# Hash attention and a mixture of adapters on one core: x turned by TensorE for fourteen pairs, proj spread by two products, and a new list of steps

## The chip, the cores and the metric

The kernel runs on one core of one Trainium2 chip. The metric is the device time of one execution in microseconds (us), the median of several runs; smaller is better. The core has five engines that work at once and meet only at semaphores: TensorE (PE in the profile, its weight loads PEld), VectorE (DVE), ScalarE (ACT), GpSimd (POOL) and SyncE (SP), which here only issues transfers. Each engine carries out its own instructions strictly in the order in which they were written, so an instruction that waits holds up everything behind it on its engine.

## The reference

Four batches of eight heads, 768 positions, 64 numbers per head. Two queries and keys may see each other only where the signs of six projections (their hash codes) are equal; the rows that the attention gives are then the input x of a mixture of eight rank-16 adapters, of which each row uses two.

```
q_bits = einsum('bhsd,dk->bhsk', q, proj) > 0          # the same for k; proj is 64 x 6
mask   = q_bucket[:, :, :, None] == k_bucket[:, :, None, :]
scores = where(mask, q @ k.T / sqrt(64), -1e9)
attn   = softmax(scores) @ v                           # (4, 8, 768, 64)
x      = attn.transpose(0, 2, 1, 3).reshape(3072, 512)
logits = x @ w_gate                                    # 8 experts, the best two with softmax weights w
out    = x + sum over the two of  w * (x @ A[e]) @ B[e]
```

## The kernel before

**Pairs.** The 32 heads are worked off as sixteen pairs of two heads, four pairs to a batch. For a pair, the rows of q and k are loaded (`Lq`, `Lk`), cast to bf16 on POOL (`Nq`, `Nk`), and turned by the crossbar, a DMA that transposes (`Xq`, `Xk`, issued by SP), into a buffer `aug` of which there are three; the second head is shifted down to the first 64 partitions by POOL or DVE (`Sk`, `Sq`). In parallel DVE turns the 32 x 32 blocks of the same rows (`Tq`, `Tk`), PE multiplies them with `hst`, a spread copy of proj (`Ha`), DVE takes the signs (`G`), and SP writes them to DRAM (`W`) and reads them back (`Rd`) into rows 64 to 69 of `aug`. A score matmul then contracts over 70 rows: 64 of the head and six of codes, so that unequal codes push a score down.

**Scores and attention.** `Sc p s` fills one of three PSUM buffers of 1024 columns, `Ex p s` is the exp of it on ACT, nine to a pair and 144 in all. `Pv` multiplies the exps with v, `U` adds a small constant row, `Nr` divides and writes x, in float32. v is loaded, cast and summed by `Lv`, `Vc` and `Vs`, the last two on POOL. The last two pairs go in six smaller pieces, whose steps end in `l` (`Pvl`, `Nl`, `Xbl`, `Xpl`, `Xcl`).

**Adapters.** x of a pair is cast to bf16 on POOL (`Xb`, L490) and has to be turned. For pairs 0 to 7 PE turns it (`Xp`, six transposes at L500) and DVE copies it out of PSUM (`Xc`, L504); for pairs 8 to 13 the crossbar does both (`Xx`, L494). When the four pairs of a batch are turned, `Lg` gives logits and low-rank products, `Mx`, `Ge`, `Gw`, `Zm`, `Sr` the gates, `Zt`, `Zc`, `De`, `St` the result, `Ou` the store.

**The start.** Pair 0 has its own way: quarters of q and k are loaded (`L0`, two by SP, two by ACT's queue), turned by PE in float32 (`T0`), copied (`FC`, `CA`), and their codes are made directly (`HH` on PE with proj, `SG0` on DVE and ACT). `Lproj` loads proj twice by SP. `hst` spreads it by eight copies of 32 x 6 numbers on DVE (L221). A few matmuls on zeros (`warm`) stand at the beginning.

**Order.** `STEPS` is a list written out by hand or by a program; `run` calls each step in turn, and that fixes the order on every engine and in every queue. `BANKS` says which PSUM pool a tile uses: `s` (three buffers, the scores and the start's tiles), `v` and `m` (one each). No scheduler reorders anything.

Of the kernel before, what the change touches and what calls it, by code (L numbers as in the profile page):

```python
# [31 lines left out]
BANKS = """
tf0=v hh0=s tf1=m hh1=s tf2=v hh2=s tf3=m hh3=s warm=s s0_0=s s0_1=s s0_2=s s0_3=s s0_4=s s0_5=s s0_6=s s0_7=s
s0_8=s pv0_0=m pv0_1=v xt0=m hs1=m s1_0=s s1_1=s s1_2=s s1_3=s s1_4=s s1_5=s s1_6=s s1_7=s s1_8=s pv1_0=m
pv1_1=v xt1=m hs2=m s2_0=s s2_1=s s2_2=s s2_3=s s2_4=s s2_5=s s2_6=s s2_7=s s2_8=s pv2_0=m pv2_1=v xt2=m hs3=m
s3_0=s s3_1=s s3_2=s s3_3=s s3_4=s s3_5=s s3_6=s s3_7=s s3_8=s pv3_0=v pv3_1=m xt3=m lz0_0=m zt0_0=m dl0_0=m
dl0_1=m dl0_2=v lz0_1=m zt0_1=m dl0_3=m dl0_4=m dl0_5=m hs4=v s4_0=s s4_1=s s4_2=s s4_3=s s4_4=s s4_5=s s4_6=s
s4_7=s s4_8=s pv4_0=v pv4_1=v xt4=m hs5=m s5_0=s s5_1=s s5_2=s s5_3=s s5_4=s s5_5=s s5_6=s s5_7=s s5_8=s
pv5_0=v pv5_1=v xt5=v hs6=v s6_0=s s6_1=s s6_2=s s6_3=s s6_4=s s6_5=s s6_6=s s6_7=s s6_8=s pv6_0=v pv6_1=v
xt6=m hs7=m s7_0=s s7_1=s s7_2=s s7_3=s s7_4=s s7_5=s s7_6=s s7_7=s s7_8=s pv7_0=v pv7_1=m xt7=m lz1_0=m  # L40
zt1_0=m dl1_0=m dl1_1=m dl1_2=m lz1_1=m zt1_1=m dl1_3=m dl1_4=v dl1_5=m hs8=m s8_0=s s8_1=s s8_2=s s8_3=s
s8_4=s s8_5=s s8_6=s s8_7=s s8_8=s pv8_0=v pv8_1=v hs9=m s9_0=s s9_1=s s9_2=s s9_3=s s9_4=s s9_5=s s9_6=s
s9_7=s s9_8=s pv9_0=v pv9_1=v hs10=v s10_0=s s10_1=s s10_2=s s10_3=s s10_4=s s10_5=s s10_6=s s10_7=s s10_8=s
pv10_0=v pv10_1=v hs11=m s11_0=s s11_1=s s11_2=s s11_3=s s11_4=s s11_5=s s11_6=s s11_7=s s11_8=s pv11_0=v
pv11_1=m lz2_0=m zt2_0=m dl2_0=m dl2_1=m dl2_2=m lz2_1=m zt2_1=m dl2_3=v dl2_4=m dl2_5=v hs12=m s12_0=s
s12_1=s s12_2=s s12_3=s s12_4=s s12_5=s s12_6=s s12_7=s s12_8=s pv12_0=v pv12_1=v hs13=m s13_0=s s13_1=s
s13_2=s s13_3=s s13_4=s s13_5=s s13_6=s s13_7=s s13_8=s pv13_0=v pv13_1=v hs14=m hs15=v s14_0=s s14_1=s
s14_2=s s14_3=s s14_4=s s14_5=s s14_6=s s14_7=s s14_8=s s14_9=s s14_10=s s14_11=s s14_12=s s14_13=s s14_14=s
s14_15=s s14_16=s s14_17=s pvl0=m xtl0=s pvl1=v xtl1=m pvl2=m xtl2=s pvl3=s xtl3=s pvl4=m xtl4=s pvl5=s xtl5=s
lz3_0=s zt3_0=v dl3_0=v dl3_1=v dl3_2=v lz3_1=s zt3_1=s dl3_3=v lz3_2=m zt3_2=s dl3_4=s lz3_3=s zt3_3=s  # L50
dl3_5=m
# [4 lines left out]
Lq 1,Nq 1,Tq 1,Wt 2,Sc 0 0,Sc 0 1,Ex 0 0,T0 3,FC 3,CA 3 1,CA 2 1,CA 3 0,CA 2 0,Nq 2,Lk 3,Lk 2,Nk 2,Lv 0,Vc 0
Xk 1,Xq 1,hst,HH 2,SG0 2 0,SG0 2 1,Sc 0 2,Ex 0 1,Ex 0 2,HH 3,SG0 3 1,SG0 3 0,Ha 1,G 1,W 1,Lv 1,Sc 0 3,Sc 0 4
Sc 0 5,Ex 0 3,Ex 0 4,Sc 0 6,Ex 0 5,Ex 0 6,Sc 0 7,Sc 0 8,Xq 2,Tq 2,Tk 2,Sq 1,Ha 2,G 2,vones,Pv 0 1 4,Ex 0 7
Ex 0 8,Sk 1,Rd 1,Sc 1 0,Pv 0 0 4,Sc 1 1,Sc 1 2,Vs 0,U 0 0,Pv 0 0 5,Ex 1 0,Ex 1 1,Ex 1 2,Nk 3,Tk 3,Xk 2,Sk 2
Lq 3,Tq 3,Nq 3,Vc 1,Vs 1,Lv 2,Vs 2,W 2,Xk 3,Lq 4,Sk 3,Nq 4,Sq 2,Rd 2,Xq 3,Sc 1 3,Pv 0 0 0,Pv 0 0 1,Pv 0 0 2  # L60
# [636 lines left out]
```

## Time and profile before

| | before |
|---|---|
| median of 3 runs | 174.94 us (173.92 to 176.3) |
| the profiled execution | 175.81 us, of which the span from first to last instruction is 174.0 us |
| PE busy | 153.6 us, 88% |
| ACT busy | 142.2 us, 82% |
| DVE busy | 118.2 us, 68% |
| POOL busy | 101.9 us, 59% |
| mean granted TensorE clock | 0.938 |
| moved by DMA | 34.15 MB, 196 GB/s |

A row of groups names the line of the kernel, the engine, the operation, out<-in with their shapes and the count; behind the first bar stand the busy time of the group and the mean of one in ns, behind the second the idle time just before it and what ended it. A row of the timeline begins with its start and its length in us and ends with the idle time before it in brackets. A row of stages gives, for each engine, its busy us in the stage (and how many instructions started), then the granted clock (1.00 is full), the DMA share and GB/s.

### The profile page before, as it was taken

How to read it: one execution, taken by the hardware profiler on the slowest of the kernel's cores; microseconds unless marked ns; L12 is line 12 of the kernel's file. 1: busy time of each engine (PE TensorE's matmuls, PEld its weight loads, DVE VectorE, ACT ScalarE, POOL GpSimd, SP SyncE). 2: the span in 40 equal slices, each digit the busy share in tenths (PEclk: the TensorE clock that was granted, in tenths of full speed). 3: DMA queues.
4: the chain of work that ended last, by engine and by line, in shares of the span. 5: the costliest groups of instructions: out<-in, count | busy, mean ns of one | idle time of the engine just before them, and what ended most of it. 6: DMA issues, size and time to landing. Idle time of an engine off the chain costs nothing.

```text
span 174.0 us, 5211 instructions
## 1 busy us (share of the span) xinstructions
PE 153.6 (88%) x2098; PEld 103.3 (59%) x2098; DVE 118.2 (68%) x302; ACT 142.2 (82%) x168; POOL 101.9 (59%) x154
## 2 busy tenths in 40 slices
...
PEclk9998555799999999999999999999999999999995
...
GB/s 183 343 237 68 106 205 221 144 84 203 189 197 198 169 175 243 230 180 252 146 236 180 206 224 277 182 216 263 205 106 302 187 191 147 255 143 146 143 308 162
DMA packets 63075, 34.15 MB, mean 196 GB/s; under 512 B 48714, under 2 KB 61130, under 8 KB 63050
## 3 DMA queue, kind: packets, MB, share of 16 engines
...
q0 software_dynamic: 4832, 0.27, 5.2%
...
q8 instruction: 16, 0.26, 0.7%
...
## 4 chain that ended last, share of the span: by engine, by line
PE 40%; DMA 29%; DVE 14%; POOL 7%; issue 3%; SPq 3%; DVEq 1%; ACT 0%; POOLq 0%
PE s L426 18%; PE pv L462 9%; DMA aug<-nb 7%; DMA vn<-in_v_dram 6%; DMA nat<-in_q_dram 6%; DMA dr<-s 5%; PE hs L383 4%; DMA xT<-xb 3%; DVE R L370 3%; DMA aug<-dr 2%; PE lz L569 2%; PE pvl L526 2%; DVE x L634 2%; POOL nb L320 2%; DVE zm L600 2%
## 5 line engine op out<-in xcount | busy, mean ns | idle before, releaser
L435 ACT ACTIVATE P<-s 128x1024 bf16<-128x1024 f32 x144 | 135.2, 1049 | 14.5 <-PE s L426 14.3
L426 PE MATMUL s<-aug 70*128 70x512 bf16 (+3 forms) x426 | 84.9, 325 | 1.7 <-DMA aug<-dr 1.2
L462 PEld LDWEIGHTS <-P 128*128 128x128 bf16 x1008 | 42.8, 100 | 14.1 <-issue 4.1
L426 PEld LDWEIGHTS <-aug 70*128 70x128 bf16 x426 | 35.6, 101 | 22.8 <-issue 8.5
L462 PE MATMUL pv<-vb,P 128*128 128x65 bf16 x1008 | 46.8, 197 | 1.4 <-DVE ri L482 1.4
L370 DVE STREAM_TRANSPOSE R<-nat 128x768 f32<-128x768 f32 x30 | 28.7, 966 | 5.0 <-DMA nat<-in_q_dram 2.9
L320 POOL CAST nb<-nat 128x768 bf16<-128x768 f32 x30 | 24.7, 828 | 11.5 <-DMA nat<-in_q_dram 7.1
L262 POOL TENSOR_TENSOR vs<-vn 128x384 f32<-128x384 f32 x16 | 16.0, 1002 | 10.7 <-DMA vn<-in_v_dram 10.5
L634 DVE SCALAR_TENSOR_TENSOR x<-dl,rt,x 128x512 f32<-128x512 f32 x24 | 17.6, 742 | 2.4 <-PE dl L627 2.2
L383 PE MATMUL hs<-R,hst 128*32 128x192 f32 x240 | 14.1, 351 | 5.9 <-DVE hst L221 3.2
L490 POOL CAST xb<-x 128x768 bf16<-128x768 f32 x14 | 11.5, 824 | 10.2 <-DVE x L484 8.7
L256 POOL CAST vb<-vn 128x768 bf16<-128x768 f32 x16 | 13.5, 845 | 6.4 <-DMA vn<-in_v_dram 6.4
L359 POOL COPY aug<-aug 64x768 bf16<-64x768 bf16 x15 | 12.4, 824 | 7.4 <-DMA aug<-nb 6.7
L484 DVE TENSOR_TENSOR x<-pv,ri 128x384 f32<-128x384 f32 x28 | 15.6, 558 | 1.0
L383 PEld LDWEIGHTS hs<-R,hst 128*32 128x32 f32 x240 | 6.7, 113 | 10.9 <-issue 6.2
L482 DVE RECIPROCAL ri<-pv 128x6 f32<-128x6 f32 x28 | 5.2, 185 | 10.3 <-PE pv L462 5.6
L359 DVE COPY aug<-aug 64x768 bf16<-64x768 bf16 x15 | 8.6, 576 | 4.8 <-DMA aug<-nb 4.4
L390 DVE TENSOR_SCALAR sg<-hs 128x192 bf16<-128x192 f32 x15 | 5.4, 357 | 9.6 <-PE hs L383 9.5
L569 PE MATMUL lz<-wa,xT 128*128 128x136 bf16 x96 | 8.4, 223 | 2.2 <-DMA xT<-xb 1.8
L627 PE MATMUL dl<-Bcat,zT 128*128 128x512 bf16 x24 | 9.0, 381 | 0.7 <-DVE x L634 0.4
L450 PE MATMUL pv<-vb,eps 128*128 128x390 bf16 x28 | 9.5, 339 | 0.0
L569 PEld LDWEIGHTS <-xT 128*128 128x128 bf16 x96 | 6.4, 97 | 4.0 <-DMA xT<-xb 2.3
...
## 6 DMA issues: line engine op xcount, KB each, us to landing
...
```

Source lines behind the costliest of these rows:

```text
L256: self.nc.gpsimd.tensor_copy(out=self.vb[p % 3][:, :, 0:self.T, 0:self.D], in_=self.vn[p])
L262: nc.gpsimd.tensor_add(out=s3, in0=vn[:, :, 0:3, :], in1=vn[:, :, 3:6, :])
L320: self.nc.gpsimd.tensor_copy(out=t.rearrange("p t h d -> p h t d"), in_=self.nat[p, c].rearrange("p h (t d) -> p h t d", t=self.T))
L359: (self.nc.vector if (p, c) in SHIFT_DVE else self.nc.gpsimd).tensor_copy(out=a[0:64, :, 2 + c, :], in_=a[64:128, :, c, :])
L370: self.nc.vector.transpose(out=t, in_=self.nat[p, c])
L383: self.nc.tensor.matmul(out=hs[32 * j:32 * j + 32], lhsT=self.hstt[:, hf].rearrange("p b i -> p (b i)"), rhs=rhs, start=(hf == 0), stop=(h ...
L426: self.nc.tensor.matmul(out=ps[:, o:o + n], lhsT=a[0:70, kt, 2 * h + 1, :], rhs=a[0:70, q0 // P:(q0 + n) // P, 2 * h, :], start=True, stop ...
L435: self.nc.scalar.activation(out=self.Pt[p + u][:, at:at + W], in_=self.ps[f"s{p}_{s}"], func=ACT.Exp, bias=-192.0, scale=64.0 if p == 0 el ...
L462: self.nc.tensor.matmul(out=pv[:, i, :], lhsT=self.Pt[p][:, o:o + P], rhs=self.vb[p % 3][:, h, kt, :], start=self.first(pv), stop=False, s ...
L484: nc.vector.tensor_tensor(out=self.x[b][:, :, c:c + D], in0=pv[:, 0:T, 0:D], in1=ri.unsqueeze(2).to_broadcast([P, T, D]), op=ALU.mult)
L569: self.nc.tensor.matmul(out=lz[:, n, :], lhsT=self.xT[b][:, t, i, :], rhs=self.wa[:, t, :], start=self.first(lz), stop=False, skip_group_c ...
L634: self.nc.vector.scalar_tensor_tensor(out=x, in0=self.ps[f"dl{b}_{i}"], scalar=self.sm["rt", b, g][:, n:n + 1], in1=x, op0=ALU.mult, op1=A ...
```

## The change

Four things are edited. First, `Xx` is no longer called: all fourteen pairs up to the fourteenth are turned by `Xp` and `Xc`, so six crossbar transposes go from SP's queue and thirty-six PE transposes and six DVE copies come in. Second, `hst` is made by two small products on PE (`hp`, into PSUM bank `m`) with a spread identity `rep`, and one DVE product with a mask `group4`; the eight copies go. `rep` and `group4` are filled at the start, by five more memsets and one of 64 x 256 on DVE and two copies on POOL. Third, `Lproj` is issued by ACT's queue. Fourth, `STEPS` and `BANKS` are new throughout; the list also has five further matmuls on zeros (`Dm`), two ahead of `Sc 0 3` and three ahead of `Sc 1 0`.

```diff
 OUT_QUEUE = ['SP', 'ACT', 'SP', 'ACT', 'SP', 'ACT']
+PROJ_QUEUE, LOAD0_QUEUE = 'ACT', ['SP', 'ACT', 'SP', 'ACT']
...
 STEPS = """
-Wt 0,L0 0,L0 1,L0 3,consts,warm 1,warm 3,warm 0,warm 4,warm 6,warm 5,T0 0,T0 1,FC 0,CA 0 0,FC 1,CA 1 0,Wt 1
...
+consts,Wt 0,L0 0,vones,L0 1,Lproj,L0 2,Lk 1,L0 3,warm 7,warm 6,warm 1,warm 4,warm 3,warm 2,warm 5,Lq 1,T0 0
...
+        self.group4 = sg.tile([P, 4], F32, name="group4")
+        nc.vector.memset(self.group4, 0.0)
+        for i in range(4):
+            nc.vector.memset(self.group4[32 * i:32 * i + 32, i:i + 1], 1.0)
...
+        self.rep = sg.tile([64, 2, 4, 32], F32, name="rep")
+        nc.vector.memset(self.rep, 0.0)
+        for f in range(2):
+            rows = slice(32 * f, 32 * f + 32)
+            nc.gpsimd.tensor_copy(out=self.rep[rows, f], in_=self.ident[rows, None, rows].broadcast_to([32, 4, 32]))
...
-            self.nc.sync.dma_start(out=self.proj3[64 * e:64 * e + 64, 0:6], in_=self.proj)
+            self.queue(PROJ_QUEUE).dma_start(out=self.proj3[64 * e:64 * e + 64, 0:6], in_=self.proj)
+
+    def hp(self):
+
+        t = self.bank("hp", [self.P, 2, 6])
+        for f in range(2):
+            self.nc.tensor.matmul(out=t[:, f], lhsT=self.rep[:, f].rearrange("p i c -> p (i c)"),
+                                  rhs=self.proj3[0:64, 0:6], start=True, stop=True)
 
     def hst(self):
-        for i in range(4):
-            for f in range(2):
-                self.nc.vector.tensor_copy(out=self.hstt[32 * i:32 * i + 32, f, 0:6, i],
-                                           in_=self.proj3[32 * f:32 * f + 32, 0:6])
+        shape = [self.P, 2, 6, 4]
+        self.nc.vector.tensor_mul(out=self.hstt[:, :, 0:6, :],
+                                  in0=self.ps["hp"][:, :, :, None].broadcast_to(shape),
+                                  in1=self.group4[:, None, None, :].broadcast_to(shape))
...
+    def Dm(self, p, s, k):
+        t = self.bank(f"s{p}_{s}", [self.P, SCORE_COLS])
+        self.nc.tensor.matmul(out=t[:, 0:512], lhsT=self.wz[:, 0:128], rhs=self.wz, start=True, stop=True)
```

What the new list does to the order is shown at three places.

DVE at the start, before: `hst` is the spread proj, `hs1` the projections of pair 1, `R01` and `R11` the turned q and k of pair 1.

```order
L313 TENSOR_SCALAR aug0_87<-hh0_144 6x3x128 x2
L370 STREAM_TRANSPOSE R11_159<-nat11_149 128x768
L370 STREAM_TRANSPOSE R01_173<-nat01_169 128x768
L288 TENSOR_SCALAR qkT_94<-tf3_185 128x384
L221 COPY hst_96<-proj3_95 32x6 x8
L313 TENSOR_SCALAR aug0_87<-hh2_215 6x3x128 x2
L390 TENSOR_SCALAR sg1_240<-hs1_231 128x192
```

The same place now, with the signs of pair 0's second head (`hh2`) behind those of pair 1:

```order
L334 TENSOR_SCALAR aug0_87<-hh0_168 6x3x128 x2
L391 STREAM_TRANSPOSE R01_176<-nat01_148 128x768
L391 STREAM_TRANSPOSE R11_178<-nat11_137 128x768
L237 TENSOR_TENSOR hst_96<-hp_197,group4_105 128x2x24
L309 TENSOR_SCALAR qkT_94<-tf3_201 128x384
L411 TENSOR_SCALAR sg1_227<-hs1_218 128x192
L414 TENSOR_SCALAR s21_229<-sg1_227 128x192
L334 TENSOR_SCALAR aug0_87<-hh2_231 6x3x128 x2
```

Eight copies have become one product, and it stands ahead of the copy of the last quarter (`tf3`).

ACT's first instructions, before and then now: `nat0` holds the quarters of pair 0, `tf0` is the first turned quarter.

```order
L271 DMA nat0_93<-in_k_dram 128x384 x2
L197 ACT_TABLE_LOAD
L286 COPY qkT_94<-tf0_126 128x384
L297 CAST aug0_87<-qkT_94 64x3x128
L311 ACTIVATE aug0_87<-hh1_151 6x3x128
```

```order
L202 ACT_TABLE_LOAD
L288 DMA nat0_93<-in_k_dram 128x384
L226 DMA proj3_95<-in_proj_dram 64x6 x2
L288 DMA nat0_93<-in_k_dram 128x384
L307 COPY qkT_94<-tf0_150 128x384
L318 CAST aug0_87<-qkT_94 64x3x128
```

The table load has moved ahead of the loads, and proj stands between the two quarters of k.

SP's queue between the codes of pair 12 (`dr12`) and of pair 13 (`dr13`), before and then now: `aug<-dr` is `Rd`, `dr<-s2` is `W`, `xT<-xb` is `Xx`.

```order
L401 DMA aug0_87<-dr12_2302 6x24x128
L243 DMA nat114_2448<-in_k_dram 128x2x384
L330 DMA_TRANSPOSE aug1_88<-nb013_2247 128x6x128
L494 DMA_TRANSPOSE xT2_1888<-xb9_2171 128x6x128
L397 DMA dr13_2595<-s213_2411 128x6x32
L330 DMA_TRANSPOSE aug2_89<-nb014_2236 128x6x128
L494 DMA_TRANSPOSE xT2_1888<-xb8_2038 128x6x128
L640 DMA out_0_dram<-x0_408 128x1024
L401 DMA aug1_88<-dr13_2595 6x24x128
```

```order
L422 DMA aug0_87<-dr12_2299 6x24x128
L418 DMA dr13_2414<-s213_2412 128x6x32
L260 DMA nat114_2504<-in_k_dram 128x2x384
L351 DMA_TRANSPOSE aug1_88<-nb013_2332 128x6x128
L661 DMA out_0_dram<-x0_434 128x1024 x2
L422 DMA aug1_88<-dr13_2414 6x24x128
```

Between the two reads of codes two crossbar transposes of x and one of pair 14 are gone, and the write of pair 13's codes follows at once.

More of the change, by code (lines that the diff above doesn't have):

```diff
@@ L37 @@
[L37 to L41, printed above, removed]
@@ L47 @@
[L47 to L51, printed above, removed]
+tf0=v hh0=s tf1=m hh1=s tf2=m hh2=s tf3=v hh3=s warm=s hp=m s0_0=s s0_1=s s0_2=s s0_3=s s0_4=s s0_5=s s0_6=s
@@ new lines @@
+s0_7=s s0_8=s pv0_0=v pv0_1=m xt0=v hs1=m s1_0=s s1_1=s s1_2=s s1_3=s s1_4=s s1_5=s s1_6=s s1_7=s s1_8=s
+pv1_0=v pv1_1=m xt1=m hs2=v s2_0=s s2_1=s s2_2=s s2_3=s s2_4=s s2_5=s s2_6=s s2_7=s s2_8=s pv2_0=v pv2_1=m
+xt2=m hs3=v s3_0=s s3_1=s s3_2=s s3_3=s s3_4=s s3_5=s s3_6=s s3_7=s s3_8=s pv3_0=v pv3_1=m xt3=m lz0_0=m
+zt0_0=m dl0_0=m dl0_1=m dl0_2=v lz0_1=m zt0_1=m dl0_3=m dl0_4=m dl0_5=m hs4=m s4_0=s s4_1=s s4_2=s s4_3=s
+s4_4=s s4_5=s s4_6=s s4_7=s s4_8=s pv4_0=v pv4_1=v xt4=m hs5=v s5_0=s s5_1=s s5_2=s s5_3=s s5_4=s s5_5=s
@@ L56 @@
[L56 to L60, printed above, removed]
```

171 lines of the change are left out of this document (90 added, 81 removed).

## The prediction

> **What bounds the kernel now.** I read the page's busy shares and slices first, then ACT's timeline, then the stages of the start, then the chain of waits.
>
> ```profile
> span 174.0 us, 5211 instructions
> PE 153.6 (88%) x2098; PEld 103.3 (59%) x2098; DVE 118.2 (68%) x302; ACT 142.2 (82%) x168; POOL 101.9 (59%) x154
> ...
> PEclk9998555799999999999999999999999999999995
> ```
>
> The profiled execution took 175.81 us, 1.81 more than its span and 0.87 above the median of 174.94. The busiest two engines are PE and ACT, and the granted clock fell to half in slices 4 to 7. ACT does 144 exps; where it does them without a pause is read from its timeline, whose rows end with the wait ahead of them:
>
> ```profile
> 9.64 2.86 ACT L435 ACTIVATE P<-s 128x1024 bf16<-128x1024 f32 x3
> 12.53 0.85 ACT L311 ACTIVATE aug<-hh 6x384 bf16<-6x384 f32 x2
> 18.06 5.61 ACT L435 ACTIVATE P<-s 128x1024 bf16<-128x1024 f32 x6 [4.68 <-PE s L426]
> 25.80 1.02 ACT L435 ACTIVATE P<-s 128x1024 bf16<-128x1024 f32 x1 [2.14 <-PE s L426]
> ...
> 35.60 14.77 ACT L435 ACTIVATE P<-s 128x1024 bf16<-128x1024 f32 x16 [0.84 <-PE s L426]
> 51.28 14.96 ACT L435 ACTIVATE P<-s 128x1024 bf16<-128x1024 f32 x16 [0.91 <-PE s L426]
> ...
> 78.59 23.50 ACT L435 ACTIVATE P<-s 128x1024 bf16<-128x1024 f32 x25
> ...
> 123.35 1.02 ACT L435 ACTIVATE P<-s 128x1024 bf16<-128x1024 f32 x1 [0.51 <-PE s L426]
> 124.86 6.54 ACT L435 ACTIVATE P<-s 128x1024 bf16<-128x1024 f32 x7 [0.49 <-PE s L426]
> 132.48 1.02 ACT L435 ACTIVATE P<-s 128x1024 bf16<-128x1024 f32 x1 [1.08 <-PE s L426]
> 133.81 1.02 ACT L435 ACTIVATE P<-s 128x1024 bf16<-128x1024 f32 x1 [0.30 <-PE s L426]
> 135.04 1.94 ACT L435 ACTIVATE P<-s 128x1024 bf16<-128x1024 f32 x2 [0.21 <-PE s L426]
> 138.86 0.22 ACT L588 ACTIVATE e<-d 128x24 f32<-128x24 f32 x1 [1.88 <-DVE d L579]
> ...
> 160.76 2.86 ACT L435 ACTIVATE P<-s 128x1024 bf16<-128x1024 f32 x3 [0.26 <-PE s L426]
> ```
>
> At its own pace an exp takes 0.94 us (23.50 over 25). The kernel is four parts: 18.06 us up to the fourth exp; 17.54 up to 35.60, in which only thirteen exps are done; 128 exps from 35.60 to 163.62, which at 0.94 would be 120.3 and take 128.0; and a tail of 10.4 to 174.0. In the third part the pauses from 123 to 139 sum to 4.47 (0.51, 0.49, 1.08, 0.30, 0.21, 1.88). So ACT is the bound in the middle, and the start and the stretch round 130 are where time lies open. Why the start stalls is in the stages (PE, its loads, DVE, ACT, POOL, then the clock) and the start's timeline:
>
> ```profile
> 14.00:15.00 1.00, 0.52 (x8) 0.19 (x8) 0.97 (x2) 0.00 (x0) 1.00 (x2) 1.00 1.29 156
> 15.00:16.00 1.00, 0.01 (x2) 0.00 (x0) 1.00 (x1) 0.00 (x0) 1.00 (x8) 0.99 0.01 1
> 16.00:17.00 1.00, 0.82 (x9) 0.22 (x10) 0.97 (x3) 0.00 (x0) 0.92 (x5) 0.50 0.00 0
> ```
>
> ```profile
> 8.78 2.03 DVE L370 STREAM_TRANSPOSE R<-nat 128x768 f32<-128x768 f32 x2 [0.27 <-DMA nat<-in_k_dram]
> 11.32 4.81 DVE L221 COPY hst<-proj 32x6 f32<-32x6 f32 x8
> 16.18 0.87 PE L383 MATMUL hs<-R,hst 128*32 128x192 f32 x8 [1.17 <-DVE hst L221]
> 18.15 0.39 SPq L397 DMA_DIRECT2D dr<-s  x1
> 20.66 0.34 SPq L401 DMA_DIRECT2D aug<-dr  x1
> 24.73 1.03 PE L426 MATMUL s<-aug 70*128 70x512 bf16 x3 [0.56 <-DMA aug<-dr]
> ```
>
> The eight copies of proj run from 11.32 to 16.13. PE stands in order behind them at `Ha 1`, with 0.53 us of work between 14 and 16; the clock drops at 16.0 and comes back only within the eighth slice, whose 0.7 puts it near 33. The codes of pair 1 then go out at 18.15, are read back from 20.66, and PE has them at 24.73. All of this hangs on `hst`.
>
> **Start, up to the first exp: later.** ACT's queue now holds a table load, a quarter of k, two loads of proj, a quarter of k.
>
> ```profile
> 0.74 0.88 ACTq L271 DMA_DIRECT2D nat<-in_k_dram  x2
> 1.64 1.28 ACT L197 ACT_TABLE_LOAD   x1 [1.64 <-PEq L681]
> 1.69 1.19 SPq L216 DMA_DIRECT2D proj<-in_proj_dram  x2
> 6.35 0.48 PE L304 MATMUL hh<-qkT,proj 64*32 64x384 f32 x1 [0.20 <-DMA proj<-in_proj_dram]
> ```
>
> Proj went out at 1.69; now it goes at 0.74 + 1.28 + 0.44 = 2.46, 0.77 later. `HH` waited for proj, so the first exp slides from 9.64 to 10.4. Bounds: 0 if the lighter SP queue makes up for it, 1.3 if the quarter of k behind the table load is what comes last. The new memsets and casts of the masks lie in the first four microseconds, in which DVE and POOL wait for loads: nothing.
>
> **Start, up to the fourth exp: the gain.** DVE's two transposes would end at 10.81 + 0.77 = 11.6. The new `hst` is one product of 48 numbers to a partition; no row has this form, and I take the median of the old copies, 0.43 us, with their least and most, 0.16 and 1.77, as bounds.
>
> ```profile
> L221 DVE COPY hst<-proj x8: 161/428/1766, 11.3 to 14.4; 32x6 f32<-32x6 f32 x8
> L304 PE MATMUL hh<-qkT,proj x16: 479/483/507, 6.3 to 12.0; 64*32 64x384 f32 x16
> ...
> 88.95 0.22 PE dl L627
> ```
>
> So `hst` stands at 12.0 and `Ha 1` ends at 12.9 (0.87). Behind it PE has `HH 2` and `HH 3` (about 0.5 each), then two `Dm` and the two 512-column halves of `Sc 0 3` (0.22 each, the full-speed product of that width in the chain): 14.8. ACT is free by 10.4 + 2.86 + 0.85 = 14.1. The fourth exp starts at 14.8, against 18.06: 3.3 less. One wait is new: `hp` uses PSUM bank `m` after the third turned quarter, so PE stands there until ACT has copied it, just ahead of the first exp at 10.4; behind it stand only a turn and `Sc 0 2`, needed at the third exp, 12.3. Hidden.
>
> **Codes of pair 1.** `Ha 1` ends at 12.9, `W` goes out 1.1 later (17.05 to 18.15 before), the read-back 2.51 after that (18.15 to 20.66): 16.5. Landing 4.07 later (20.66 to 24.73) is 20.6, and the exp some 0.8 behind (1.07 on the slow PE), 21.4; ACT has finished pair 0 at 14.8 + 5.61 = 20.4. Against 25.80 that is **4.4 less in all up to here** (2.5 if POOL or a load is late, 5.5 if ACT alone counts).
>
> **Pair 1.** Seven exps from 25.80 to 35.60 took 9.80 on a half-speed PE; at 0.94 they take 6.6: **3.2 less**, if the clock stays full. In the new order PE has no gap above about 0.5 us between 10 and 18, and the five `Dm` fill the wait ahead of pair 1; they cost nothing there, five times 0.22 = 1.1 if the cover is gone.
>
> [...]
>
> **The stretch from 123 to 139.** The chain runs through SP's queue:
>
> ```profile
> 116.98 4.47 DMA dr<-s
> ...
> 122.34 5.47 DMA aug<-nb
> ...
> 131.44 5.72 DMA xT<-xb
> ```
>
> The last is the crossbar turning x: `Lg 2 0` waits for it on PE, and 1.88 of ACT's pause follows. It goes, and the other five crossbar turns leave the queue that carried the late codes. What is late next is the round trip of pair 12's codes (`Ha 12` stands at the same exp as before), about 1.0 of the 4.47. **3.0 less** (0 to 4.5).
>
> **PE's new work.**
>
> ```profile
> 97.35 0.34 PE xt L500 x6
> L504 DVE COPY xT<-xt 128x768 bf16<-128x768 bf16 x8 | 4.4, 553 | 2.4 <-PE xt L500 2.4
> ```
>
> Six more turns are 2.0 us of PE and 3.3 of DVE. DVE is 68% busy and not the bound; its cover gone, the copies delay `Lg` by 0.55 each. PE is as busy as ACT or busier, yet ACT kept 0.94 in the stretch from 78.59 with turns in it, the one at 97.35 among them. I take half: **1.0 more** (0 to 3).
>
> **The new order elsewhere.** A new list makes its own waits; the old one has two of 0.9 in the clean part (51.28 above is one). I take one more, **0.8 more** (−1 to 4). At the end, `St 3 1`, 0.66 to 0.74 us on a busy DVE, moves ahead of the last `Nl` but one: **0.5 less** (1.3 less to 0.5 more).
>
> ```profile
> 163.62 0.74 DVE L634 SCALAR_TENSOR_TENSOR x<-dl,rt,x 128x512 f32<-128x512 f32 x1
> ```
>
> **Sum.** −4.4 − 3.2 − 3.0 + 1.0 + 0.8 − 0.5 = −9.3, so 175.81 becomes 166.5; less the 0.87 by which that execution lies above the median, **165.6 us**.
>
> **Rivals.**
>
> *The clock drops all the same* (0.17). PE waits for loads from 4 to 7 us and for the codes near 20; one of these waits may be enough. Then the 3.2 is not gained, and `Ha` and the scores of pair 0 take twice as long, about 1 more: 169.8. For it: one quiet stretch was enough, for 17 us. Against: there is no pause as long as that one. [...]
>
> *The middle does not gain* (0.16). If the pauses round 130 come from the round trip of the codes and not from the turns of x, 3.0 stays: 168.6. For it: two of the three legs of that chain are codes and q or k. Against: the longest wait, 1.88, has the crossbar's 5.72 right ahead.
>
> *PE stands behind POOL* (0.06, slower). In the new list `Xp` mostly follows its `Xb` directly. PE works in order: if POOL gets to `Xb` only then, PE loses a cast at every turn.
>
> ```profile
> L490 POOL CAST xb<-x 128x768 bf16<-128x768 f32 x14 | 11.5, 824 | 10.2 <-DVE x L484 8.7 <-issue 1.4
> ```
>
> Fourteen times 0.82 and 0.1 of semaphore is 12.9: 178.5. It outweighs the gain from ten such stops on. Against: `Xb 7` and `Xp 7` stood together before, and PE's rows show no wait for a cast; POOL is 59% busy and idle 10.2 us ahead of these casts, 8.7 of them until x itself is there.
>
> **Chances and range.** The sum as it stands has 0.61. Its own terms reach from 161 (the start at 5.5, the middle at 4.5, PE's work hidden) to 170 (the middle at 0 and a late start); the first two rivals lie inside up to 171.5. The range 161 to 172 leaves out about 2 in 10: the slower rival, a cold clock with a bad middle, and a list still better than I take it. What a measurement can tell from no change is about 2%, here below 171.4 or above 178.4. Faster: nearly all of the first case and about three quarters of the next two, 0.83; within 2% 0.12; slower 0.05.
>
> **What would show it.** Right: the fourth exp near 14.8, the tenth near 21.4, granted clock full from 10 to 35, no pause of ACT near the turns of pairs 8 to 11, and last exp about 10 us earlier. Wrong: a clock of 0.5 anywhere before 35; PE idle ahead of L521, the new line of the turns, until POOL's cast; ACT's pauses summing to more than 5 us after pair 2; or a first exp later than 11.

## The result and the profile after

| | before | after |
|---|---|---|
| median of 4 runs | 174.5 us (173.92 to 176.3) | 169.01 us (165.7 to 170.72) |
| the profiled execution, its span | 175.81, 174.0 us | 167.52, 165.7 us |
| PE busy | 153.6 us | 150.4 us |
| ACT busy | 142.2 us | 141.8 us |
| mean granted clock of that execution | 0.938 | 0.981 |

The kernel is faster, by a ratio of 0.9531 (95% interval 0.9379 to 0.9684). This ratio and every one below leave out executions over 1.5% above the fastest of their kernel, which in the changed kernel are those with the lower granted clock, while the medians hold all executions, so the text argues from medians, clocks and traces.

The head of the page after; the granted clock has no dip until the tail:

```profile
span 165.7 us, 5292 instructions
...
PE 150.4 (91%) x2143; PEld 102.5 (62%) x2143; DVE 116.8 (71%) x307; ACT 141.8 (86%) x168; POOL 103.5 (62%) x156
...
PEclk9999999999999999999999999999999999999975
```

ACT's timeline after (start, length, the exps in the row, and in brackets the wait ahead of them):

```profile
9.42 2.86 ACT L456 ACTIVATE P<-s 128x1024 bf16<-128x1024 f32 x3
13.44 0.86 ACT L332 ACTIVATE aug<-hh 6x384 bf16<-6x384 f32 x2 [1.15 <-PE hh L325]
14.40 21.55 ACT L456 ACTIVATE P<-s 128x1024 bf16<-128x1024 f32 x23
36.81 9.27 ACT L456 ACTIVATE P<-s 128x1024 bf16<-128x1024 f32 x10 [0.86 <-PE s L447]
47.66 11.51 ACT L456 ACTIVATE P<-s 128x1024 bf16<-128x1024 f32 x12 [1.57 <-PE s L447]
...
109.33 5.80 ACT L456 ACTIVATE P<-s 128x1024 bf16<-128x1024 f32 x6 [1.29 <-PE s L447]
...
152.93 2.86 ACT L456 ACTIVATE P<-s 128x1024 bf16<-128x1024 f32 x3 [0.34 <-PE s L447]
```

The fourth exp starts at 14.40 (18.06 before), and from there 23 exps run without a pause. The tenth is the seventh of that row, 14.40 + 6 x 0.94 = 20.0 (25.80 before). At 36.81 the changed kernel begins its 27th exp. Before, the row of sixteen exps from 35.60 begins with the 17th, so its 27th is the eleventh there, at 35.60 + 10 x 0.93 = 44.9. The start has given 8.1 us.

Cutting both traces at that exp and at the end of the last one gives two stages for each kernel (length, then the busy us of PE, its loads, DVE, ACT and POOL, then the granted clock, DMA share and GB/s); before, then after:

```profile
44.90:163.62 118.72, 111.15 (x1721) 80.48 (x1719) 87.14 (x229) 110.92 (x126) 73.66 (x102) 1.00 0.93 197
163.62:174.00 10.38, 3.80 (x33) 1.86 (x32) 6.51 (x31) 1.86 (x9) 0.00 (x0) 0.79 0.67 255
```

```profile
36.81:155.79 118.98, 113.04 (x1758) 82.05 (x1757) 90.16 (x234) 111.13 (x125) 76.04 (x106) 1.00 0.87 196
155.79:165.70 9.91, 3.97 (x35) 1.78 (x32) 6.34 (x30) 2.01 (x9) 0.00 (x0) 0.68 0.50 190
```

The same 118 exps take 118.72 and 118.98: the middle has given nothing, with PE 1.9 us busier in it. The tail gave 0.5. So 8.1 - 0.3 + 0.5 = 8.3, the difference of the two spans.

Where the start comes from is in its timeline after:

```profile
0.73 1.28 ACT L202 ACT_TABLE_LOAD   x1 [0.73 <-PEq L702]
0.77 0.40 ACTq L288 DMA_DIRECT2D nat<-in_k_dram  x1
1.21 1.16 ACTq L226 DMA_DIRECT2D proj<-in_proj_dram  x2
...
10.45 0.21 DVE L237 TENSOR_TENSOR hst<-hp,group 128x48 f32<-128x48 f32 x1
11.12 0.86 PE L404 MATMUL hs<-R,hst 128*32 128x192 f32 x16
12.69 0.37 SPq L418 DMA_DIRECT2D dr<-s  x1
16.59 0.34 SPq L422 DMA_DIRECT2D aug<-dr  x1
...
19.47 0.61 PE L447 MATMUL s<-aug 70*128 70x512 bf16 x3
```

`Ha 1` (the row of `hs`) runs at 11.12 instead of 16.18, and ahead of `HH 2` and `HH 3`; the codes of pair 1 go out at 12.69 (18.15 before) and PE works on them at 19.47 (24.73 before).

In the middle, pauses of the old order went and others came: from the 27th exp to the last, ACT's pauses sum to 7.5 us before and 7.3 after. The chain after names what two of the longer ones wait for: codes of pair 11 (the pause of 1.29 at 109.33), and k of pair 15, on which DVE stands ahead of the gates of batch 2 (a pause of 1.52 at 130.66).

```profile
104.63 3.95 DMA aug<-dr
...
123.61 5.59 DMA nat<-in_k_dram
```

### The profile page after: what moved, and what is told of

Same layout as the page of the kernel before. It is cut to its first block, busy times and chain, and to the rows that moved or that the text cites. A ratio compares the mean times of both kernels' runs of the same rounds, so it can differ in the third digit from the quotient of the medians.

```text
span 165.7 us, 5292 instructions
## 1 busy us (share of the span) xinstructions
PE 150.4 (91%) x2143; PEld 102.5 (62%) x2143; DVE 116.8 (71%) x307; ACT 141.8 (86%) x168; POOL 103.5 (62%) x156
## 4 chain that ended last, share of the span: by engine, by line
PE 45%; DMA 20%; DVE 16%; POOL 11%; issue 4%; SPq 1%; ACT 1%; POOLq 0%; DVEq 0%
PE s L447 21%; PE pv L483 11%; DMA aug<-dr 8%; DMA nat<-in_k_dram 6%; DVE x L655 5%; PE hs L404 4%; DMA nat<-in_q_dram 4%; POOL nb L341 3%; PE pv L471 2%; DMA aug<-nb 2%; PE lz L590 2%; PE xt L521 2%; DVE R L391 2%; POOL aug L380 2%; PE pvl L547 1%
## 5 line engine op out<-in xcount | busy, mean ns | idle before, releaser
L447 PE MATMUL s<-aug 70*128 70x256 bf16 (+3 forms) x426 | 79.7, 310 | 5.3 <-DMA aug<-dr 3.3
L447 PEld LDWEIGHTS <-aug 70*128 70x128 bf16 x426 | 34.8, 97 | 24.8 <-issue 8.9
L483 PEld LDWEIGHTS <-P 128*128 128x128 bf16 x1008 | 39.8, 97 | 10.2 <-issue 2.6
L483 PE MATMUL pv<-vb,P 128*128 128x65 bf16 x1008 | 43.1, 193 | 0.4 <-DVE x L655 0.3
L404 PE MATMUL hs<-R,hst 128*32 128x192 f32 x240 | 12.9, 332 | 0.1
L648 PE MATMUL dl<-Bcat,zT 128*128 128x512 bf16 x24 | 9.6, 400 | 1.1 <-ACT zT L643 0.7
L380 DVE COPY aug<-aug 64x768 bf16<-64x768 bf16 x15 | 8.0, 535 | 3.3 <-DMA aug<-nb 2.8
L525 DVE COPY xT<-xt 128x768 bf16<-128x768 bf16 x14 | 7.7, 552 | 3.6 <-PE xt L521 3.5
L521 PE MATMUL xt<-ident_bf,xb 128*128 128x128 bf16 x84 | 7.0, 219 | 1.6 <-DVE ri L503 1.2
```

The costliest lines, as they stand in the source:

```text
L380: (self.nc.vector if (p, c) in SHIFT_DVE else self.nc.gpsimd).tensor_copy(out=a[0:64, :, 2 + c, :], in_=a[64:128, :, c, :])
L404: self.nc.tensor.matmul(out=hs[32 * j:32 * j + 32], lhsT=self.hstt[:, hf].rearrange("p b i -> p (b i)"), rhs=rhs, start=(hf == 0), stop=(h ...
L447: self.nc.tensor.matmul(out=ps[:, o:o + n], lhsT=a[0:70, kt, 2 * h + 1, :], rhs=a[0:70, q0 // P:(q0 + n) // P, 2 * h, :], start=True, stop ...
L483: self.nc.tensor.matmul(out=pv[:, i, :], lhsT=self.Pt[p][:, o:o + P], rhs=self.vb[p % 3][:, h, kt, :], start=self.first(pv), stop=False, s ...
```

## The experiments

The question is which part brought the 8.3, and where the 3.0 forecast for the stretch round 130 went. The runs were made in three groups; the median of the kernel before beside them was 174.77, 175.65 and 175.26. Differences between runs of different groups carry the difference of these as well.

| kernel | median (range), runs | before beside it | mean clock of its runs |
|---|---|---|---|
| before, hst by products | 173.24 (171.09 to 174.68), 10 | 174.77 | 0.947 |
| before, wait filled | 174.32 (171.32 to 176.95), 4 | 174.77 | 0.952 |
| changed, eight copies | 172.59 (168.67 to 174.23), 4 | 174.77 | 0.946 |
| changed, no `Dm` | 168.71 (168.65 to 174.34), 4 | 174.77 | 0.960 |
| before, hst by products and early | 170.32 (167.63 to 176.2), 4 | 175.65 | 0.950 |
| the same again | 170.7 (168.96 to 172.04), 6 | 175.26 | 0.958 |
| the same, x turned by PE | 173.69 (170.42 to 176.03), 12 | 175.26 | 0.967 |
| changed, x by the crossbar | 184.86 (182.74 to 186.65), 4 | 175.65 | 0.927 |
| changed, k earlier | 170.02 (169.41 to 175.84), 4 | 175.65 | 0.960 |
| changed, list mended | 172.16 (168.5 to 173.94), 10 | 175.65 | 0.962 |
| changed, again (the control) | 169.9 (166.53 to 175.25), 6 | 175.26 | 0.964 |
| changed, scores first | 168.86 (165.7 to 169.8), 6 | 175.26 | 0.971 |

Ratios to before: hst by products 0.9882 (0.9825 to 0.9939), wait filled 0.9883 (0.9734 to 1.0033), no `Dm` 0.9674 (0.9594 to 0.9753), hst early 0.9733 (0.9578 to 0.9887) and again 0.9803 (0.9725 to 0.9882), its x by PE 0.9866 (0.9795 to 0.9937), k earlier 0.9855 (0.9743 to 0.9967), list mended 0.9823 (0.9635 to 1.0012), scores first 0.9581 (0.9499 to 0.9662).

### hst alone, in the old list

`hp`, `hst` and the two masks are those of the changed kernel, `hp` in bank `m`; of the list only this place changes:

```diff
-    ...,Xk 1,Xq 1,hst,HH 2,...
+    ...,Xk 1,Xq 1,hp,hst,HH 2,...
```

> The kernel before with one part of the change alone: hst by two products on PE (bank m) and one on DVE; old list, proj by SP, x of pairs 8 to 13 by the crossbar. Theory (the gain is the start, and hst is its whole cause): Ha 1 ends near 13.4 instead of 17.05, fourth exp near 14.5 (18.06 before), tenth near 22 (25.80), clock full from 10 to 35, exps of pair 1 at 0.94: 6 to 7.5 us less than before, about 167.5. Rival (the new list brings it, hst alone only shifts the wait to the codes): fourth exp early, but tenth exp later than 24 and the clock still falling, 0 to 2.5 us less.

It brought 1.5 us at the median, not 6 to 7.5. PE's and ACT's timeline of this run:

```profile
13.54 0.86 PE L400 MATMUL hs<-R,hst 128*32 128x192 f32 x16
22.27 0.61 PE L443 MATMUL s<-aug 70*128 70x512 bf16 x3 [2.71 <-DMA aug<-dr]
...
22.92 3.05 ACT L452 ACTIVATE P<-s 128x1024 bf16<-128x1024 f32 x3 [2.33 <-PE s L443]
```

The stall at `Ha 1` is gone: it runs at 13.54, and the fourth exp came at 14.98. But `Ha 1` still stands behind `HH 2`, `Sc 0 2` and `HH 3`, so the codes of pair 1 arrive after ACT has run out, and PE waits 2.71 us for them. The stages there, cut in lengths of 3.41 us (columns as in the stages above; the third number from the end is the granted clock):

```profile
19.43:22.84 3.41, 0.69 (x13) 0.43 (x9) 1.36 (x3) 1.15 (x2) 0.00 (x0) 1.00 1.22 162
22.84:26.25 3.41, 3.41 (x24) 1.89 (x22) 1.86 (x2) 2.96 (x3) 2.84 (x4) 0.50 1.16 320
26.25:29.68 3.43, 3.43 (x40) 2.47 (x39) 0.75 (x2) 2.05 (x2) 3.12 (x6) 0.50 0.64 150
29.68:33.10 3.42, 3.42 (x64) 2.34 (x62) 1.84 (x5) 2.59 (x3) 3.29 (x5) 1.00 0.21 75
```

PE worked 0.69 us in the length ahead of 22.84, and the clock then fell for two lengths. In this run the quiet stretch has moved from `hst` to the codes and the drop of the clock with it: the rival's way and size, though the tenth exp, at 22.92, came earlier than the rival had it.

### The copies back, in the new list

`hst` is the eight copies on DVE again, `hp` and the masks go:

```diff
-    hp,hst,T0 3,FC 3,...
+    hst,T0 3,FC 3,...
```

> The changed kernel with hst made by the eight copies on DVE again (no hp, no masks), all else as changed. Theory: DVE is at the copies from about 10.4 to 15.2, PE stands at Ha 1, the clock drops near 15 to 16 and stays at half for some 17 us; fourth exp near 17, 26 exps done only near 43 instead of 35.95: 5 to 7.5 us more than the changed kernel, near 175. Rival (the new list carries the gain): 0.5 to 2 us more, since the list has other work for PE.

In the profiled run the clock fell at 12.20, and the fourth exp came late:

```profile
10.65 2.42 DVE L222 COPY hst<-proj 32x6 f32<-32x6 f32 x8
...
19.09 20.27 ACT L440 ACTIVATE P<-s 128x1024 bf16<-128x1024 f32 x22 [0.96 <-PE s L431]
...
43.22 20.43 ACT L440 ACTIVATE P<-s 128x1024 bf16<-128x1024 f32 x22 [2.25 <-PE s L431]
```

The fourth exp came at 19.09. The 27th exp is at 43.22, 6.4 later than in the changed kernel, as the theory had it for this run, but not by the theory's one drop of some 17 us: the clock fell at 12.20 for two lengths, and again at 39.52 and 114.60. The median is 2.7 to 3.6 above the two medians of the changed kernel, between the theory and the rival. The eight copies took 2.42 us here and 4.81 in the old order, which makes the stall half as long; why they differ is open. Together with the run before it: hst is worth 1.5 in the old list and some 3 in the new one, and the new list without it 2.2 (174.77 to 172.59). Neither is the whole gain, and by these medians the two parts are worth more together than apart.

### The wait of before filled

`Fl` is a product on zeros, 448 columns wide, into a bank that is free there:

```diff
-    ...,SG0 3 0,Ha 1,G 1,...
+    ...,SG0 3 0,Fl 0,...,Fl 15,Ha 1,G 1,...
```

> The kernel before with sixteen matmuls on zeros (448 columns, 0.2 us each) on PE straight ahead of Ha 1, where PE waits for the eight copies from 12.5 to 16.2; nothing else is changed. Theory (stall and clock are two terms; the quiet stretch of PE starts the drop): clock stays full, fourth exp at 17.3 to 18.1, pair 1 at 0.94 to an exp, 3 to 4.5 us less than before. Rival A (exps of pair 1 are held by codes and v, not by the clock): clock full, time 0 to 1 less. Rival B (the clock drops for another cause): 0.5 still from 16 to 33, time as before to 0.5 more.

The filler did its work, PE was busy from 12.04 to 16.7, and the clock did not fall at 16.0. It fell at 21.18:

```profile
17.77:21.18 3.41, 2.54 (x24) 1.14 (x25) 2.40 (x4) 3.41 (x5) 1.91 (x4) 1.00 0.28 26
21.18:24.59 3.41, 1.25 (x18) 0.49 (x10) 1.45 (x3) 1.79 (x2) 0.00 (x0) 0.50 1.26 217
```

So the quiet stretch at `hst` goes with the drop of before, as supposed, but filling that stretch alone does not keep the clock: it stayed at half for three lengths. The codes of pair 1 came no sooner either, since the copies are still there: the tenth exp was at 26.41 (25.80 before), with PE at full clock until 21.18. The time is 0.5 lower at the median, within what can be told, and that is rival A's size. In this run the term for the clock did not come without the term for the codes.

### No `Dm`

```diff
-    HH 3,SG0 3 1,Dm 0 3 1,Dm 0 3 0,Sc 0 3,...,Dm 1 0 2,Dm 1 0 1,Dm 1 0 0,Rd 1,...
+    HH 3,SG0 3 1,Sc 0 3,...,Rd 1,...
```

> The changed kernel without its five matmuls on zeros (Dm), two ahead of Sc 0 3 and three ahead of Sc 1 0. Theory (real work fills PE from 10 to 18, the Dm cost and bring nothing): clock full to 35, time within 0.5 us of the changed kernel. Rival (they hold the clock over the wait for pair 1's codes near 17 to 19.5): a clock of 0.5 from near 19 to 33 or so, 2 to 4 us more.

168.71 us, as the theory had it; the clock was full from 10.82 to the tail. The kernel leaves out products on zeros that nothing reads. Four runs don't exclude that they help now and then.

### hst early, in the old list

```diff
-    Ex 0 0,T0 3,FC 3,...,Xk 1,Xq 1,hp,hst,HH 2,SG0 2 0,SG0 2 1,Sc 0 2,Ex 0 1,Ex 0 2,HH 3,SG0 3 1,SG0 3 0,Ha 1,G 1,W 1
+    Ex 0 0,hp,hst,T0 3,FC 3,...,Xk 1,Xq 1,Ha 1,G 1,HH 2,SG0 2 0,SG0 2 1,Sc 0 2,Ex 0 1,Ex 0 2,HH 3,SG0 3 1,SG0 3 0,W 1
```

> The kernel before with hst by products, as in the run on that, and besides hp and hst ahead of the last quarter's turn (T0 3) and Ha 1, G 1 ahead of HH 2, Sc 0 2 and HH 3, as the new list has it; the rest of the old list stays. Theory (the start is one chain, and the order of the list ahead of Ha 1 carries the part that hst alone did not bring: PE then waited 2.71 us for the codes of pair 1 and the clock fell for 6.82 us): Ha 1 ends near 12 instead of 14.4, PE's wait for the codes falls to about 0.5 to 1, the clock stays full, the tenth exp comes at 20.5 to 21, the seventeenth near 28 (32.45 with hst alone, 35.60 before): 168 to 169.5 us. Rival (the gain of the changed kernel past hst comes from the middle of the new list): about as with hst alone, 172 to 173.5.

```profile
14.12 1.02 ACT L452 ACTIVATE P<-s 128x1024 bf16<-128x1024 f32 x1 [2.49 <-PE s L443]
15.17 0.86 ACT L328 ACTIVATE aug<-hh 6x384 bf16<-6x384 f32 x2
16.05 30.36 ACT L452 ACTIVATE P<-s 128x1024 bf16<-128x1024 f32 x33
46.85 6.52 ACT L452 ACTIVATE P<-s 128x1024 bf16<-128x1024 f32 x7 [0.44 <-PE s L443]
```

The fourth exp is 1.65 later than in the changed kernel, since `Sc 0 2` now stands behind `Ha 1`, but then 33 exps run without a pause. By 46.41 it has done 36 exps; the changed kernel has done 36 by 46.08. The span of this run was 166.0, that of the changed kernel's profile 165.7. The median, 170.32, lies above the theory's 168 to 169.5 and below the rival's 172. With `hst`, `Ha 1` and `G 1` moved and hst by products, everything else old, the x turns on the crossbar included, the old kernel is close to the changed one, as its second measurement confirms:

> The kernel before with hst by products and Ha 1 ahead of HH 2, once more on the same chip as the changed kernel. Theory (the gain of the change is hst and the order ahead of Ha 1, and the rest of the new list brings nothing): median within 1.5 us of the changed kernel's. Rival (the rest of the list and the turns bring what the forecast said, 1.7 in all: 3.0 and 0.5 less, 1.8 more): 1.5 to 3 us above the changed kernel.

170.7 against 169.9 for the control beside it; the medians of all ten runs of each are the same two numbers. The clock is not safe in this kernel either: in the profiled execution of the repeat it fell at 13.08 for one length and at 19.92 for three, and the tenth exp came at 24.28. Of the 5.4 us between the control and before (169.9 to 175.26), 4.6 come with `hst` and the order ahead of `Ha 1`. What the rest of the new list and the turns of x bring between them is 0.8, no more than can be told.

### x by the other way, in either list

The changed kernel with the crossbar again, shown for pair 8, and so for pairs 9 to 13:

```diff
-    ...,Xb 8,Xp 8,Sq 12,Xc 8,...
+    ...,Xb 8,Sq 12,Xx 8,...
```

> The changed kernel with x of pairs 8 to 13 turned by the crossbar again: each of the six Xc becomes Xx at its place in the list, and Xp goes. Theory (the place of the turns is worth little in the new list: its pauses there come from late loads and codes): pauses of ACT between 96 and 156 within 1.5 us of the changed kernel's, 168 to 170.5. Rival A (the forecast's: the crossbar's queue costs 3): 171.5 to 173, with a pause ahead of Ge 2 0 that the chain puts down to xT<-xb. Rival B (PE's six turns cost more than they bring): 166.5 to 168.

None of them: 15 us slower. What SP waits for between 100 and 165 (sum, times, longest):

```profile
SPq L515 <- POOL xb L511: 9.2, 2, 7.5
SPq L515 <- POOL vs L279: 5.1, 1, 5.1
```

At the place of `Xc` the crossbar turn has to wait on SP for POOL's cast, and every load and code behind it in SP's queue waits too. Part of the 15 us is clock: it fell five times before the tail. The opposite edit, in the old list with hst early:

```diff
-    ...,Xx 9,W 13,Xq 14,Xx 8,...,Ou 2 0,Xx 12,Lg 3 0 0,Xx 13,Lg 3 0 2,...
+    ...,Xp 9,Xc 9,W 13,Xq 14,Xp 8,Xc 8,Xb 11,...,Ou 2 0,Xp 12,Xc 12,Lg 3 0 0,Xp 13,Xc 13,Lg 3 0 2,...
```

> The kernel of the run beside it (old list, hst early), and besides x of pairs 8 to 13 by TensorE and DVE: each Xx becomes Xp and Xc at its place, banks m, m, m, v, v, v, with Xb 11 and the turn of pair 11 moved up a few steps so that PE does not stand for POOL's cast. It is the part of the change on x alone. Forecast's terms (3.0 less at the stretch, 1.0 more for PE): the pause at Ge 2 0 (1.61 with the crossbar here) goes, 1.5 to 2.5 us less than the run beside it. Rival A (the pause is replaced by the next wait, codes or loads, as in the changed kernel): within 0.8 of the run beside it. Rival B (PE is the bound there and pays 2.0 for the turns): 1 to 2 us more.

3.0 slower than the run beside it, more than rival B's size, and no run shows its reason, PE as the bound. The pause at `Ge 2 0` did not go: it is 1.37, and 1.20 in the trace of the run beside it. Two other pauses of ACT are longer than there, one of 1.78 at 130.67 (0.20 there) and one of 2.62 (none of its kind there), whose rows are:

```profile
153.25 0.49 PE L518 MATMUL xt<-ident_bf,xb 128*128 128x128 bf16 x6 [0.64 <-DVE x L652]
153.78 0.56 DVE L522 COPY xT<-xt 128x768 bf16<-128x768 bf16 x1 [0.58 <-PE xt L518]
154.40 0.35 PE L587 MATMUL lz<-wa,xT 128*128 128x136 bf16 x3 [0.65 <-DVE xT L522]
...
155.12 0.56 DVE L522 COPY xT<-xt 128x768 bf16<-128x768 bf16 x1 [0.78 <-PE xt L518]
...
156.69 0.22 ACT L606 ACTIVATE e<-d 128x24 f32<-128x24 f32 x1 [2.62 <-DVE d L597]
```

At the place of `Xx` the turn now stands in PE's order right ahead of the logits that need it. Turn, copy, logits, turn, copy, logits follow each other between PE and DVE, and ACT waits 2.62 for the gate. The crossbar's turn stood at the same place of the list, but SP gets there well before PE does: in the trace of before SP issued these two at 148.28 and 152.77, and the logits ran at 157.84. So the two edits of the change, x and list, can't be priced one at a time by swapping a step at its place, and together they are worth about nothing in the middle.

### The pauses of the new list

```diff
-    Lq 14,Xb 9,...,Lq 15,Tk 13,...,Lk 14,Tk 14,Xq 13,...,Lk 15,Nk 15,Tk 15
+    Lq 14,Lk 14,Xb 9,...,Lq 15,Lk 15,Tk 13,...,Tk 14,Xq 13,...,Nk 15,Tk 15
```

> The changed kernel with two loads of k moved up in SP's queue: Lk 14 behind Lq 14 and Lk 15 behind Lq 15, some 11 and 16 us sooner; nothing else. Theory (the pause of 1.52 us at Ge 2 0 is DVE at Tk 15, waiting for k of pair 15): DVE's wait of 2.03 us at Tk 15 and ACT's pause at Ge 2 0 go; the codes of pair 12 and 13, which share the queues with the loads, come up to 0.5 later: 0.5 to 1.5 us less than the changed kernel, near 168. Rival (the pause is PE's load: the pause only moves to the next exp): the wait at Tk 15 goes and the time stays, 169.

The pause at `Ge 2 0` was not there, but nor was it in the control and in the run with the scores first, which have k where the changed kernel has it; it comes and goes from one execution to the next, and so the run can't show what moving the loads does to it. The time is that of the changed kernel, 170.02. This run's trace shows something else, early on:

```profile
35.15 0.79 DVE L380 COPY aug<-aug 64x768 bf16<-64x768 bf16 x1 [2.69 <-DMA aug<-nb]
...
36.78 0.80 PE L521 MATMUL xt<-ident_bf,xb 128*128 128x128 bf16 x6 [2.38 <-DVE ri L503]
```

```profile
32.95:36.36 3.41, 1.45 (x14) 0.67 (x9) 1.18 (x3) 3.41 (x4) 2.67 (x4) 1.00 1.47 191
36.36:39.77 3.41, 2.99 (x24) 1.38 (x24) 2.38 (x5) 1.16 (x2) 2.38 (x3) 0.50 0.81 169
```

DVE stands at `Sq 3` until the crossbar has turned q of pair 3, and behind it is `Nr 1 0`, which frees the bank that `Xp 0` needs; so PE stands at the first turn of x, and in this run the clock fell there for three lengths. In the changed kernel's own trace the same wait is 1.17 and the clock held:

```profile
33.97 0.49 PE L521 MATMUL xt<-ident_bf,xb 128*128 128x128 bf16 x6 [1.17 <-DVE ri L503]
```

Next, four places at once: those of the diff, besides `Sq 11` ahead of two `St`, and `Lk 14`, `Lk 15` as above.

```diff
-    Pv 1 1 3,Xq 3,Sq 3,Pv 1 0 5,Nr 1 0   ...   Xq 4,Sq 4   ...   Nk 5,Wt 5   ...   Xk 4,Sk 4   ...   Lk 6,...,Lq 6,Tq 6,Rd 4
+    Pv 1 1 3,Xq 3,Pv 1 0 5,Nr 1 0,Sq 3   ...   Xq 4,Xk 4,Sq 4   ...   Sk 4,Nk 5,Wt 5   ...   Rd 4,Lk 6,...,Lq 6,Tq 6
```

> The changed kernel with the two loads moved up as in the run beside it, and four steps more, each at a pause of ACT: Sq 3 behind Nr 1 0 (DVE stood 2.10 us at Sq 3, and PE behind it at Xp 0: pause of 0.86 at 36.8), Xk 4 and Sk 4 earlier and Rd 4 ahead of the loads Lk 6 and Lq 6 (codes of pair 4: 1.57 at 47.7), Sq 11 ahead of two St on DVE (codes of pair 11: 1.29 at 109.3). Theory (the middle was not lost to PE's added work but to these waits of the new list, each of which can be taken away): three of the four pauses go, 2.5 to 4 us less than the changed kernel, 165 to 166.5. Rival (PE is the bound between the pauses, and what is saved at one comes back at the next): the pauses move, 0 to 1 less.

The rival's side, and worse: 172.16. The pause at 36.8 went, and a longer one came right behind:

```profile
36.33 0.40 SPq L422 DMA_DIRECT2D aug<-dr  x1
...
40.05 1.02 ACT L456 ACTIVATE P<-s 128x1024 bf16<-128x1024 f32 x1 [2.10 <-PE s L447]
```

`Xk 4` had been put ahead of `Rd 3` in SP's queue, and the codes of pair 3 went out at 36.33 instead of 33.25. The new stop comes from that one step, so this run does not tell whether the pauses can be taken away. The next tries the first of them. Beside it the changed kernel ran once more:

> The changed kernel itself, as a control on the same chip as the three beside it. Its times so far lie in two groups, 165.7 and 167.5 with a mean granted clock of 0.98 and 170.5 and 170.7 with 0.95. Theory (what sets its spread is whether the clock falls for one to three windows of 3.41 us near 36 to 47, where PE stands at Xp 0 and then for the codes): median 168 to 171, and each run's time follows its mean clock, about 0.8 us for each us of clock lost. Rival (something else, the loads' time in DRAM): times that do not follow the clock.

> The changed kernel with three steps of the list moved at its first turn of x: Sc 2 7 ahead of Xp 0 and Ex 2 5, Sc 2 8 ahead of Ha 4, so that PE has scores to do where it stood for 1.2 us near 33 (DVE at Sq 3, the turned q of pair 3, and the bank of Xp 0 behind it). Theory (that stop is what ACT's pause of 0.86 at 36.8 comes from, and what lets the clock fall in some runs): the pause goes; runs with a mean clock under 0.96 become fewer; median 0.5 to 2 us under the changed kernel's. Rival (the codes of pair 3 and 4 are late next, by the same transfers): the pause moves to Ex 3 0, median within 0.5.

```diff
-    Sc 2 6,Xb 0,Xp 0,Xc 0,Nk 4,Sc 2 7,Ha 4,...,Ex 2 5,Ex 2 6,Ex 2 7,Pv 2 0 0,Pv 2 0 3,Pv 2 0 5,Sc 2 8,Ex 2 8
+    Sc 2 6,Xb 0,Sc 2 7,Xp 0,Xc 0,Nk 4,Ex 2 5,Sc 2 8,Ha 4,...,Ex 2 6,Ex 2 7,Pv 2 0 0,Pv 2 0 3,Pv 2 0 5,Ex 2 8
```

```profile
20.35 19.51 ACT L456 ACTIVATE P<-s 128x1024 bf16<-128x1024 f32 x21 [0.55 <-PE s L447]
...
34.10 0.49 PE L521 MATMUL xt<-ident_bf,xb 128*128 128x128 bf16 x6 [0.15 <-DVE x L505]
```

PE's wait at `Xp 0` is 0.15 here and was 1.17, ACT's pause of 0.86 is gone (21 exps run without one from 20.35, the 27th among them), and the median is 168.86 against 169.9 for the control. One of six runs has a mean clock under 0.96, against two of six. Only the kernel without `Dm`, 168.71, has a lower median; 1.0 us over six runs each is a lean, not a proof. Nor do the traces prove that the edit took the pause away, for in the control, with the list unchanged, both were small too:

```profile
22.28 15.70 ACT L456 ACTIVATE P<-s 128x1024 bf16<-128x1024 f32 x17 [1.32 <-PE s L447]
38.18 9.27 ACT L456 ACTIVATE P<-s 128x1024 bf16<-128x1024 f32 x10 [0.20 <-PE s L447]
```

The exp at 38.18 is the control's 27th, and PE waited 0.37 at `Xp 0` there.

### What the clock does to the times

All ten executions of the changed kernel, with the time that its clock lost, (1 - mean clock) x span: the least lost 2.0 us and took 166.53, the most lost 11.3 and took 175.25. A straight line through the ten gives 0.88 us of time for each us lost (correlation 0.94); the 42 executions of before give 0.73 (0.70). On average before lost 12.6 and the changed kernel 5.9. The difference, 6.7, at 0.73 to 0.88 is 4.9 to 5.9 us, and the medians differ by 5.4. If these slopes held from one kernel to another, the gain would be nearly all clock that is not lost. They don't always: the kernel with the wait filled lost 8.2 where before beside it lost 11.8, and was 0.5 faster, not 2.6 to 3.2; the old list with x turned by PE lost 5.6, no more than the changed kernel, and took 173.69. So the share of the clock in the gain is not shown. Within the changed kernel the control bears out its theory on the spread, though the drop in its profiled execution lay at 111.8 and not near 36 to 47. It is no second explanation beside the waits: the drops came behind 3.41 us in which PE stood for 0.75 to 2.88 (the last section), and these figures don't part the two.

## Why the prediction was right, and where not

The median of 169.01 lies in the range and on the forecast side, 3.4 above the 165.6. The start carried it; the middle gave none of its part, and several misses at the start cancelled, as follows.

**First exp.** Forecast 10.4, measured 9.42. The step "now it goes at 0.74 + 1.28 + 0.44 = 2.46" failed: ACT's queue issued its loads from 0.77 on, beside the table load that ran from 0.73 to 2.01, and proj went out at 1.21. The control issued them at the same times and had 10.37, with PE waiting 0.97 for proj; the landing varies by as much as the term, so neither 9.42 nor 10.37 speaks for the step.

**`hst` and the fourth exp.** `hst` took 0.21, below the 0.43 taken and within its bounds; the fourth exp came at 14.40, forecast 14.8. That it lies so near is in part luck. `Ha 1` ended 0.9 before its forecast (11.98), but from there to the fourth exp it took 2.4 and not 1.9. The working had `HH 2` and `HH 3` at 0.5 each, which is the time of one of the four products of a step; the row of both is 1.48. And it let the scores come last, where ACT first had to make the signs of `HH 3` (13.44).

**Codes of pair 1.** The gain of 4.4 up to the tenth exp was 5.8 (25.80 to 20.0); with the 3.2 of pair 1 and the new pause of 0.86 that makes the 8.1. The read-back went out at 16.59 (forecast 16.5), but PE worked on the codes 2.88 later and not 4.07, so ACT alone counted, which is the working's upper bound. This too is luck of the profiled execution: in five other traces of the new list with `hst` by products it took 3.57 to 3.82, and in these and the control ACT paused 0.55 to 1.32 ahead of the tenth exp, which in the control came at 22.28. There the codes end the wait, as the working had it.

**"All of this hangs on `hst`"** failed as a cause, though not as a sum. The working itself put `HH 2` and `HH 3` behind `Ha 1`, as the new list does, and credited that to `hst`. Alone `hst` brought 1.5; with `hst` and `Ha 1` early it was 4.6. What the sentence leaves out is the order: with `Ha 1` still behind three other steps the codes came 2.33 us after ACT had run out, and the clock fell after that stop of PE as it had after the first.

**Pair 1, 3.2 less if the clock stays full.** It did in the profiled execution. This was sized as a thing that happens or not at one place. The traces show a clock that falls at a later stop of PE, near 23, 36, 40 or 112 according to kernel and execution, or not at all; four of the ten executions of the changed kernel have a mean clock of 0.954 or less. That the profiled execution lay 0.87 above the median before was taken over for the change; it lay 1.5 below its median after, and that is 2.4 of the 3.4. Which execution is profiled is chance.

**The stretch from 123 to 139, 3.0 less**: failed. With 1.0 for PE and 0.8 for the order the middle was to give 1.2 and gave -0.3. The crossbar's turn did go as a wait, and the gate of batch 2 paused 1.52 in the profile after, for k of pair 15. In the six other traces of the new list with x turned by PE that gate does not pause at all, against 1.20 to 2.63 in the five of the old list with the crossbar; what was won there was lost at other waits of the new list, for codes above all (1.57 at 47.66 and 1.29 at 109.33). Whether PE's 1.9 more in that stage costs time of its own no run tells. This is the size of the rival that "the middle does not gain", and it accounts for the other 1.0: the profiled execution took 167.52, not 166.5 (1.5 lost here, 0.5 gained at the start and 0.0 in the tail).

**The slower rival, PE behind POOL at each turn.** Not so: PE waits 1.6 us at L521 in all, none of it put down to POOL. Its weight loads wait 3.4, of which 2.0 are put down to POOL, 1.4 of these at `Xp 0`, where PE waits for DVE as well. POOL idled 2.7 ahead of the casts. The 0.1 taken for a semaphore was 0.05 at the turn that waits for its own cast: the cast ended at 69.49 and the first weights went in at 69.54. The one long stop at a turn is that at `Xp 0`, and the run with the scores first leans to its costing 1 us.

**The tail** gave 0.5, as forecast.

**The signs.** The fourth exp and the full clock from 10 to 35 came as named, and the tenth exp 1.4 earlier still. Against the forecast, the last exp was 7.8 us earlier and not about 10, there were pauses near the turns of pairs 8 to 11 (1.29 and 1.52), and ACT's pauses after pair 2 sum to 7.3, over the 5 that was named as a sign of being wrong. It pointed at the right part, the middle.
